# Scores cut from two PSUM banks by ScalarE, probabilities turned by VectorE alone, and a second square on ScalarE, in an attention-and-MLP kernel

## The chip, the cores and the metric

The kernel runs on one core of one Trainium2 chip. The metric is the device time of one execution in microseconds (us); the median over several runs counts.

## What is computed

Attention of 4 batches, 8 heads, 576 positions, head size 64, then two MLPs on the 2304 tokens, all in float32:

```python
scores = scale * np.matmul(q, k.transpose(0, 1, 3, 2))
rel = pos[:, None] - pos[None, :]
mask_local = (rel >= 0) & (rel < stride)                 # heads 0 to 3, stride = 32
mask_strided = (rel >= 0) & (pos[None, :] % stride == pos[:, None] % stride)   # heads 4 to 7
scores = np.where(masks[None, :, :, :], scores, -1000000000.0)
scores = scores - np.max(scores, axis=-1, keepdims=True)
attn = np.exp(scores)
attn = attn / (np.sum(attn, axis=-1, keepdims=True) + 1e-09)
x = np.matmul(attn, v)                                   # to 2304 tokens of 512
r = np.maximum(x @ w_in, 0.0); x = (r * r) @ w_out       # MLP 1, 512 -> 2048 -> 512
h = x @ w_in; g = h / (1.0 + np.exp(-1.702 * h)); out = g @ w_out      # MLP 2
```

A query of a local head sees at most 32 keys, a query of a strided head at most 18.

## The kernel before

**Attention.** The masks are used: the work is cut into 28 groups of 8 heads' or rows' worth of small score matrices. A strided group holds eight matrices in which 4 x 18 queries meet 4 x 18 keys, of which only the four 18 x 18 blocks on the diagonal count. A local group holds eight matrices of 96 queries by 128 keys, of which a query sees 32. Seven groups make a batch: four strided, three local. Groups 14 to 17 and 21 to 24 are strided, 18 to 20 and 25 to 27 local. Per group: `load` (DMA of q, k, v), `att_turn` (transposes of q and k into `qkT`), `att_S` (eight pairs of matmuls into two PSUM banks `ps_att`), mask and maximum (`att_max`), exponential (`att_exp`), division by the sum (`att_norm`), transposition of the probabilities, and `att_PV`, whose result goes through casts (L563, L566) into the MLP's input `xr`.

From group 14 (`n >= NTR`) q and k are turned on DVE. A strided group's scores are masked by eight DVE instructions that read PSUM (L401), and its probabilities are turned by four DVE transposes (L472) into a zeroed tile `pt`. A local group's scores are masked by eight custom DVE instructions (L421) that also give the maxima, its exponentials are eight ACT instructions (L443) that also give the sums, and its probabilities are turned by eight PE transposes (`att_P`, L483) into PSUM and copied out by two DVE copies (L493).

**MLP 1.** Each float32 operand is split in a high and a low part of PE's fast type, so a product is three matmuls. Tokens come in blocks `i` of 512, 512, 256, 512 and 512; the hidden layer in 16 steps `f`. A step is 12 matmuls into `ps_h` (L583), then the activation: ACT takes the relu (`t`, L612) and its square rounded to the high part (`gh`, L613), then `t` is squared once more (DVE, L617; ACT at L615 once `lpool` exists, from block 3), and DVE subtracts to get the low part (`gl`, L618). One step later `second` does 8 matmuls with `gh` and 4 with `gl` into the four banks `ps_acc` (L645). `t` has one buffer, `gh` and `gl` two; the two `ps_h` banks are shared with `att_PV`. At the end of blocks 0 and 1 `spill_x2` copies the four `ps_acc` banks (L700: banks 0 and 2 by DVE, 1 and 3 by ACT) into one tile with two places, and each copy leaves by a DMA; banks 2 and 3 wait for the DMAs of banks 0 and 1.

**Order.** Groups 0 to 13 and block 0 are in a hand-written front part. Groups 14 to 27 lie within the 32 steps of blocks 1 and 2: a table `AT` gives for each group the step of its scores, of its transposition and of its PV (group 18: steps 8, 9, 10; group 26: 24, 26, 28). In these blocks PE runs in program order, while DVE, ACT, GpSimd (POOL) and SyncE (SP) are put in order by a scheduler. From step (3, 0) PE, DVE and ACT run in program order. Blocks 3 and 4 also prepare the weights of MLP 2, which are loaded by DMA from then on; MLP 2 follows.

Of the kernel before, what the change touches and what calls it, by code (L numbers as in the profile page):

```python
# [22 lines left out]
def kernel(  # L23
# [176 lines left out]
    mloc = apool.tile([QT, 2, P], F32, name="mloc")  # L200
    mstr = apool.tile([SR, SR], F32, tag="mstr", name="mstr", bufs=1)
    mtri = []
# [26 lines left out]

    def shape(n):  # L230

        R, N = rows(groups[n][1])
        return (P, N, P) if n >= NTR and N == SR else (R, N, P)

# [141 lines left out]
    def att_S(n, tag, z=0):  # L376
        b, c, g = groups[n]
        R, N, _ = shape(n)
        ps = [bank(tag), bank(tag)]
        idle(ps[0], z)  # L380
        for j in range(4):
            qT, kT = tiles_qk(n, j)
            for i in range(2):
                d = slice(i * D, (i + 1) * D)
                nc.tensor.matmul(ps[i][0:R, j * P:j * P + N], qT[d], kT[d], start=True, stop=True)  # L385
        g_t[n] = ps

    def att_max(n):
        b, c, g = groups[n]
        R, N, step = shape(n)  # L390
        ps = g_t[n]
        if R == P:

            pr = abuf(n, [P, 8 * P], "pr", 1, 3)[:, 0:8 * 32].rearrange("p (x k) -> p x k", x=8)
            st = abuf(n, [P, 2, 8], "st", 1, 3)
            nc.gpsimd.memset(pr, 0.0)
            for i in range(2):
                s = ps[i].rearrange("p (j k) -> p j k", j=4)
                for r in range(4):
                    p, k0 = slice(32 * r, 32 * (r + 1)), NS * r  # L400
                    nc.vector.tensor_tensor(  # L401
                        out=pr[p, 4 * i:4 * i + 4, 0:NS], in0=s[p, :, k0:k0 + NS],
                        in1=mtri[0][p].unsqueeze(1).to_broadcast([32, 4, NS]), op=ALU.add,
                    )
            x, m = pr[:, :, 0:NS], st[:, 0, :]
            nc.vector.tensor_reduce(out=m, in_=x, op=ALU.max, axis=mybir.AxisListType.X)
            nc.vector.tensor_tensor(out=x, in0=x, in1=m.unsqueeze(2).to_broadcast([P, 8, NS]), op=ALU.subtract)
            g_t[n] = [pr, st, None]
            return
        pr = abuf(n, [P, 8 * P], "pr", 1, 3)[0:R, 0:8 * step].rearrange("p (i j k) -> p i j k", i=2, j=4)  # L410
        st = abuf(n, [P, 2, 8], "st", 1, 3)
        for j in range(4):
            for i in range(2):
                x = 4 * i + j
                if c >= 2:
                    m = mstr
                elif n < NTR:
                    m = mloc[:, 0 if g == 0 and i == 0 else 1, :]
                else:
                    m = mloc[:, 0 if (g, j) in ((0, 0), (1, 2)) else 1, :]  # L420
                nc.vector.tensor_tensor_reduce(  # L421
                    out=pr[:, i, j, 0:N], in0=ps[i][0:R, j * P:j * P + N], in1=m,
# [5 lines left out]
    def load_tri():  # L428
        mtri.append(apool.tile([P, SR], F32, tag="mstr", name="mtri", bufs=1)[:, 0:NS])
        nc.gpsimd.memset(mtri[0], -BIG)  # L430
        for r in range(0, P, 32):
            nc.sync.dma_start(mtri[0][r:r + NS], c_mstr.rearrange("(p r) (x y) -> r y p x", r=4, y=4)[0, 0])

    def att_exp(n, js=range(4)):
        R, N, _ = shape(n)
        pr, st, _ = g_t[n]
        if R == P:
            nc.scalar.activation(pr[:, :, 0:NS], pr[:, :, 0:NS], AF.Exp, scale=SCALE)
            return
        for j in js:  # L440
            for i in range(2):
                x = 4 * i + j
                nc.scalar.activation(  # L443
                    pr[:, i, j, 0:N], pr[:, i, j, 0:N], AF.Exp,
# [3 lines left out]
    def att_norm(n):  # L448
        R, N, _ = shape(n)
        pr, st, _ = g_t[n]  # L450
        if R == P:
            p = pr[:, :, 0:NS]
            N = NS
            nc.vector.tensor_reduce(out=st[:, 1, :], in_=p, op=ALU.add, axis=mybir.AxisListType.X)
        else:
            p = pr.rearrange("p i j k -> p (i j) k")[:, :, 0:N]
        nc.vector.tensor_scalar_add(st[0:R, 1, :], st[0:R, 1, :], 1e-9)
        nc.vector.reciprocal(st[0:R, 1, :], st[0:R, 1, :])
        nc.vector.tensor_tensor(
            out=p, in0=p, in1=st[0:R, 1, :].unsqueeze(2).to_broadcast([R, 8, N]), op=ALU.mult,  # L460
        )

    def att_turn_p(n):


        pr = g_t[n][0]
        pt = apool.tile([P, 2, DM], F32, tag="tmp0", name="pt", bufs=1).rearrange("p a n -> p (a n)")
        pt = pt.rearrange("p (x r k) -> p x r k", x=8, r=4)
        nc.gpsimd.memset(pt, 0.0)
        for r in range(4):  # L470
            p = slice(32 * r, 32 * (r + 1))
            nc.vector.transpose(pt[p, :, r], pr[p])  # L472
        g_t[n][2] = pt

    def att_P(n, tag, z=0):
# [20 lines left out]
    def att_PV(n, tag, z=0):  # L496
# [819 lines left out]
```

## Time and profile before

| | |
|---|---|
| median of 3 runs | 875.06 us (874.41 to 876.12) |
| profiled execution, its own time | 874.62 us |
| its span in the profile | 872.9 us |
| mean granted clock of PE | 0.999 of full speed |
| PE busy | 852.2 us, 98% of the span |
| DVE busy | 644.0 us, 74% |
| ACT busy | 462.7 us, 53% |
| POOL busy | 24.3 us, 3% |

The span is what the profile covers of the execution; the 1.7 us beside it lie around it. Times in the rows are microseconds from the span's start. Blocks 1 and 2, in which groups 14 to 27 are worked on, begin at 155.13 (first matmul L583 of step (1, 0)) and end at 328.42 (first matmul of step (3, 0)).

### The profile page before, as it was taken

How to read it: one execution, taken by the hardware profiler on the slowest of the kernel's cores; microseconds unless marked ns; L12 is line 12 of the kernel's file. 1: busy time of each engine (PE TensorE's matmuls, PEld its weight loads, DVE VectorE, ACT ScalarE, POOL GpSimd, SP SyncE). 2: the span in 40 equal slices, each digit the busy share in tenths (PEclk: the TensorE clock that was granted, in tenths of full speed). 3: DMA queues.
4: the chain of work that ended last, by engine and by line, in shares of the span. 5: the costliest groups of instructions: out<-in, count | busy, mean ns of one | idle time of the engine just before them, and what ended most of it. 6: DMA issues, size and time to landing. Idle time of an engine off the chain costs nothing.

```text
span 872.9 us, 15792 instructions
## 1 busy us (share of the span) xinstructions
PE 852.2 (98%) x5675; PEld 759.3 (87%) x5681; DVE 644.0 (74%) x1314; ACT 462.7 (53%) x1015; POOL 24.3 (3%) x49
## 2 busy tenths in 40 slices
PE   8999999999999999999989999999999999999998
PEld 5678787788888888888867899999999999999998
DVE  5999996776679656777858768788546797356853
ACT  7988896223522435555636645555344555344442
POOL 0000001110111000000000000000000000000000
PEclk9999999999999999999999999999999999999999
DMA  8997321222123206888888589987998597986673
GB/s 206 303 318 240 61 40 28 77 47 46 35 48 93 48 2 203 267 265 264 305 321 287 179 281 395 382 277 246 313 352 252 161 335 263 349 272 204 198 252 106
DMA packets 173508, 181.58 MB, mean 208 GB/s; under 512 B 71192, under 2 KB 128504, under 8 KB 171896
## 3 DMA queue, kind: packets, MB, share of 16 engines
q1 hardware_dynamic: 173432, 180.59, 64.9%
q8 instruction: 45, 0.74, 0.3%
q14 instruction: 31, 0.25, 0.1%
HBM read 141.75 MB, written 38.80 MB: 207 GB/s over the span
## 4 chain that ended last, share of the span: by engine, by line
PE 73%; DMA 11%; DVE 9%; ACT 3%; issue 1%; SPq 1%; POOL 0%; DVEq 0%; ACTq 0%
PE ps_acc L645 17%; PE ps_h L583 16%; PE ps_acc L1086 15%; PE ps_att L851 9%; PE ps_h L1086 6%; PE ps_h L851 5%; DMA stg<-in_moe_w_out_dram 4%; DMA stage<-in_moe_w_out_dram 2%; PE ps_acc L851 2%; DMA stg<-in_moe_w_in_dram 2%; PE ps_att L385 2%; ACT pr L443 1%; DVE tmp L154 1%; PE ps_h L507 1%; DVE tmp L158 1%
## 5 line engine op out<-in xcount | busy, mean ns | idle before, releaser
L583 PE MATMUL ps_h<-xr,whl 128*128 128x512 f32 (+1 forms) x948 | 211.2, 371 | 0.0
L583 PEld LDWEIGHTS ps_h<-xr,whl 128*128 128x128 f32 x948 | 164.4, 188 | 31.4 <-DVE whl L187 0.5
L645 PE MATMUL ps_acc<-gh,whl 128*128 128x512 f32 (+1 forms) x640 | 147.5, 372 | 5.0 <-ACT gh L613 2.8
L645 PEld LDWEIGHTS ps_acc<-gh,whl 128*128 128x128 f32 x640 | 111.3, 189 | 26.5 <-ACT gh L613 3.9
L645 PE MATMUL ps_acc<-gl,whl 128*128 128x512 f32 (+1 forms) x320 | 79.2, 369 | 2.6 <-DVE gl L618 2.6
L612 ACT ACTIVATE t<-ps_h 128x512 f32<-128x512 f32 (+1 forms) x64 | 34.6, 540 | 84.0 <-PE ps_h L583 73.1
L622 ACT ACTIVATE gh<-hs 128x384 f32<-128x384 f32 x72 | 37.8, 525 | 63.3 <-DVE hs L1022 63.3
L645 PEld LDWEIGHTS ps_acc<-gl,whl 128*128 128x128 f32 x320 | 56.6, 188 | 13.6 <-DVE gl L618 3.6
L443 ACT ACTIVATE pr<-pr,st 96x128 f32<-96x128 f32 (+1 forms) x160 | 59.4, 380 | 8.7 <-DVE st L421 8.7
L851 PE MATMUL ps_att<-xop,wst 128*128 128x384 f32 x288 | 58.8, 338 | 0.2
L851 PE MATMUL ps_att<-xop 128*128 128x384 f32 x288 | 58.1, 336 | 0.3 <-ACT hs L1030 0.3
L1086 PE MATMUL ps_acc<-misc,gop 128*128 128x256 f32 x432 | 54.2, 283 | 0.0
L1022 DVE TENSOR_TENSOR hs<-ps_h,hs 128x384 f32<-128x384 f32 x49 | 27.2, 556 | 35.4 <-ACT hs L1030 24.5
L1086 PEld LDWEIGHTS ps_acc<-misc,gop 128*128 128x128 f32 x432 | 53.2, 191 | 0.0
L1072 ACT CAST gop<-misc 128x768 fp32r<-128x768 f32 x42 | 34.7, 834 | 34.6 <-PE ps_acc L1086 19.0
L1072 ACT CAST gop<-g 128x768 fp32r<-128x768 f32 x42 | 34.8, 834 | 34.1 <-PE ps_acc L1086 19.8
L1025 DVE TENSOR_TENSOR gop<-g,gop 128x768 fp32r<-128x768 f32 x42 | 40.2, 956 | 16.9 <-ACT gop L1072 16.9
L851 PEld LDWEIGHTS ps_att<-xop,wst 128*128 128x128 f32 x288 | 51.0, 187 | 0.9 <-ACT hs L1030 0.9
L851 PEld LDWEIGHTS ps_att<-xop 128*128 128x128 f32 x288 | 50.4, 188 | 1.3 <-ACT hs L1030 1.2
L771 ACT CAST wst<-tmp 128x1792 fp32r<-128x1792 f32 x14 | 23.7, 1695 | 50.9 <-DVE tmp L757 43.0
L1025 DVE TENSOR_TENSOR gop<-misc,gop 128x768 fp32r<-128x768 f32 x42 | 39.9, 957 | 13.8 <-ACT gop L1072 13.7
L774 DVE TENSOR_TENSOR wst<-tmp,wst 128x1792 fp32r<-128x1792 f32 x14 | 28.4, 2025 | 26.0 <-ACT wst L771 26.0
(150 smaller groups left out, 1485.2 us busy)
## 6 DMA issues: line engine op xcount, KB each, us to landing
xop<-w2d SPq DMA_DIRECT2D x84, 256.0 KB
wst<-w2d SPq DMA_DIRECT2D x84, 256.0 KB
xop<-wo2d SPq DMA_DIRECT2D x63, 256.0 KB
w2d<-wst SPq DMA_DIRECT2D x16, 896.0 KB
misc<-wo2d SPq DMA_DIRECT2D x12, 1024.0 KB
wo2d<-wst SPq DMA_DIRECT2D x12, 896.0 KB
wx<-wo2d SPq DMA_DIRECT2D x36, 256.0 KB
stg<-in_moe_w_in_dram SPq DMA_DIRECT2D x16, 512.0 KB
```

Of the source, the lines that this page charges most:

```text
L443: nc.scalar.activation(pr[:, i, j, 0:N], pr[:, i, j, 0:N], AF.Exp, bias=st[0:R, 0, x:x + 1], scale=-1.0, accum_out=st[0:R, 1, x:x + 1],)
L583: nc.tensor.matmul(ph[:, 0:nb], w[:, kk * P:(kk + 1) * P], x[:, kk], start=(kk == KS[0] and w is ih and x is xh), stop=(kk == KS[-1] and x ...
L612: nc.scalar.activation(t, ph[:, 0:nb], AF.Relu)
L622: nc.scalar.activation(t, h, AF.Sigmoid, scale=1.702)
L645: nc.tensor.matmul(acc[c][:, 0:nb], w[:, c * P:(c + 1) * P], x, start=(f == 0 and w is oh and not lo), stop=(f == NF - 1 and lo == 1),)
L771: nc.scalar.copy(wh[:, x], t[:, x])
L774: nc.vector.tensor_tensor(out=wl[:, x], in0=t[:, x], in1=f32(wh)[:, x], op=ALU.subtract)
L851: nc.tensor.matmul(ps[:, 0:NH], w[:, a, k * P:(k + 1) * P], x[:, b + k], start=start and y == 0, stop=y == len(prods) - 1, skip_group_chec ...
L1022: nc.vector.tensor_tensor(out=h, in0=ps, in1=h, op=ALU.add)
L1025: nc.vector.tensor_tensor(out=out, in0=a, in1=b, op=op)
L1072: nc.scalar.copy(hi, g)
L1086: nc.tensor.matmul(part(ps, m), g, w[1 + h], start=j in (0, 1, 3) and p == 0 and m != 1 and not last and h == 0, stop=p == NP - 1 and last ...
```

## The change

For groups 14 to 27 the path from scores to turned probabilities is new. The two banks of scores are one tile (`bank2`). `att_cut`: ACT copies from both banks at once the block of keys that a set of 32 queries can see (strided: four copies of 32 x (8 x 18), local: three copies of 32 x (8 x 64)) into `pr`. `att_soft`: DVE adds a mask (`mwin`, loaded by eight DMAs), takes the maxima and subtracts them; one ACT instruction takes the exponentials; DVE sums, adds 1e-9, takes reciprocals and multiplies. `att_turn_p`: one DVE transpose turns all 32 x 32 blocks, and ACT copies them (strided four, local six copies) into the zeroed tile `pt`, from other partitions than those to which they go. PE turns no probabilities of these groups any more, and PE's score matmul of a strided group has 114 instead of 128 stationary columns. `att_turn(n + 1)` and `load(n + 2)` stand at the end of the step instead of in its middle. The second square of block 1 is done by ACT. The pair of `ps_att` banks is one tile in groups 0 to 13 as well, and two tiles again from step (3, 0).

```diff
+    def bank2(tag):
+        if tag == "att":
+            t = pool2.tile([P, 2, 512], F32, tag="att", name="ps_att", bufs=1)
+            pairs[:] = [t]
+            return [t[:, 0], t[:, 1]]
+        return [bank(tag), bank(tag)]
...
     def att_S(n, tag, z=0):
         b, c, g = groups[n]
-        R, N, _ = shape(n)
-        ps = [bank(tag), bank(tag)]
+        R, N = rows(c)
+        if n >= NTR and c >= 2:
+            R = 3 * 32 + NS
+        ps = bank2(tag)
...
+    def window(n):
+        if groups[n][1] >= 2:
+            return NS, 32, P, P, [(slice(32 * r, 32 * r + (32 if r < 3 else NS)), NS * r) for r in range(4)]
+        return 64, 64, QT, QT, [(slice(32 * a, 32 * a + 32), 32 * a) for a in range(3)]
...
+    def att_cut(n):
+        W, room, _, _, blocks = window(n)
+        t = apool.tile([P, 2, 8 * 64], F32, tag="pr", name="pr", bufs=1)[:, :, 0:8 * room]
+        t = t.rearrange("p o (x k) -> p o x k", x=8)
+        pr = t[:, 0]
+        s = pairs[0].rearrange("p i (j k) -> p (i j) k", j=4)
+        if room > W:
+            nc.gpsimd.memset(pr, 0.0)
+        for p, k0 in blocks:
+            nc.scalar.copy(pr[p, :, 0:W], s[p, :, k0:k0 + W])
+        g_t[n] = t
+
+    def att_soft(n):
...
+        each(mwin[c >= 2][0:R].unsqueeze(1).to_broadcast([R, 8, W]), ALU.add)
+        if c < 2 and g < 2:
+            nc.vector.memset(pr.rearrange("p (i j) k -> p i j k", i=2)[0:32, :, 2 * g, 0:32], -BIG)
+        nc.vector.tensor_reduce(out=m, in_=x, op=ALU.max, axis=mybir.AxisListType.X)
+        each(row(m), ALU.subtract)
+        nc.scalar.activation(x, x, AF.Exp, scale=SCALE)
+        nc.vector.tensor_reduce(out=z, in_=x, op=ALU.add, axis=mybir.AxisListType.X)
+        nc.vector.tensor_scalar_add(z, z, 1e-9)
+        nc.vector.reciprocal(z, z)
+        each(row(z), ALU.mult)
...
     def att_turn_p(n):
-        pr = g_t[n][0]
+        W, room, R, nq, _ = window(n)
+        pr, tu = (g_t[n][0:R, o].rearrange("p x k -> p (x k)") for o in range(2))
+        nc.vector.transpose(tu, pr)
+        tu = tu.rearrange("p (x e q) -> p x e q", x=8, q=32)
         pt = apool.tile([P, 2, DM], F32, tag="tmp0", name="pt", bufs=1).rearrange("p a n -> p (a n)")
-        pt = pt.rearrange("p (x r k) -> p x r k", x=8, r=4)
+        pt = pt[:, 0:8 * nq].rearrange("p (x q) -> p x q", x=8)
         nc.gpsimd.memset(pt, 0.0)
-        for r in range(4):
-            p = slice(32 * r, 32 * (r + 1))
-            nc.vector.transpose(pt[p, :, r], pr[p])
-        g_t[n][2] = pt
+        w = min(W, 32)
+        for a in range(0, nq, 32):
+            for e in range(room // 32):
+                k = a + 32 * e
+                nc.scalar.copy(pt[k:k + 32, :, a:a + w], tu[a:a + 32, :, e, 0:w])
+        g_t[n] = pt
...
-        if lpool:
+        if lpool or i == 1:
             nc.scalar.activation(t, t, AF.Square)
...
             for n in steps[0]:
                 att_S(n, "att")
-                att_max(n)
+                att_cut(n)
             ph = bank("h")
             mm_h(i, f, ph, KS)
             for n in steps[0]:
-                att_exp(n)
-                att_norm(n)
-                if n + 1 < len(groups):
-                    att_turn(n + 1)
-                    load(n + 2)
+                att_soft(n)
             for n in steps[1]:
-                if groups[n][1] >= 2:
-                    att_turn_p(n)
-                else:
-                    att_P(n, "att")
-                    att_pt(n, [nc.vector.tensor_copy] * 2)
+                att_turn_p(n)
...
             second(*prev)
             prev = (i, f)
+            for n in steps[0]:
+                if n + 1 < len(groups):
+                    att_turn(n + 1)
+                    load(n + 2)
```

How this moves instructions is seen at three places. In these rows a line number is that of the kernel named, `x12` a count, and `out<-in` the tiles; L615, L677 and L538 of the changed kernel are L583, L645 and L507 of before.

First, PE in block 1, around the PV of the first local group (18). Before:

```order
L583 MATMUL ps_h<-xr,whl 128x512 x12
L483 MATMUL ps_att<-ident,pr 128x96 x8
L645 MATMUL ps_acc<-gh,whl 128x512 x8
L645 MATMUL ps_acc<-gl,whl 128x512 x4
L507 MATMUL ps_h<-pr,ldv 64x96 x8
L385 MATMUL ps_att<-qkT 96x128 x8
L583 MATMUL ps_h<-xr,whl 128x512 x12
```

And now:

```order
L615 MATMUL ps_h<-xr,whl 128x512 x12
L677 MATMUL ps_acc<-gh,whl 128x512 x8
L677 MATMUL ps_acc<-gl,whl 128x512 x4
L538 MATMUL ps_h<-pt,ldv 64x96 x8
L395 MATMUL ps_att<-qkT 96x128 x8
L615 MATMUL ps_h<-xr,whl 128x512 x12
```

The eight transposes into `ps_att` between a step's `ps_h` and `ps_acc` matmuls are gone, and the PV follows the `ps_acc` matmuls of the step directly.

Second, ACT in block 1, around the same kind of group. Before, with eight exponentials ahead of a relu:

```order
L443 ACTIVATE pr,st<-pr,st 96x128 x8
L612 ACTIVATE t<-ps_h 128x512
L613 ACTIVATE gh<-t 128x512
L612 ACTIVATE t<-ps_h 128x512
L613 ACTIVATE gh<-t 128x512
```

And now, for one local group from its cut (L462) to its copies into `pt` (L503), with the relu L644, the rounded square L645 and the second square L647 of the steps between:

```order
L462 COPY pr<-ps_att 32x512 x3
L644 ACTIVATE t<-ps_h 128x512
L645 ACTIVATE gh<-t 128x512
L483 ACTIVATE pr<-pr 96x512
L647 ACTIVATE t<-t 128x512
L644 ACTIVATE t<-ps_h 128x512
L503 COPY pt<-pr 32x8x32 x6
L645 ACTIVATE gh<-t 128x512
```

The six copies into `pt` stand behind the relu of the step at whose end PV needs them, and ahead of that step's squares.

Third, the end of block 1 on DVE, where the `ps_acc` banks are copied away. Before:

```order
L617 TENSOR_TENSOR t<-t 128x256
L618 TENSOR_TENSOR gl<-t,gh 128x256
L700 COPY tmp<-ps_acc 128x512
L401 TENSOR_TENSOR pr<-ps_att,mtri 32x4x18 x8
L312 STREAM_TRANSPOSE qkT<-ld 128x2x4x4x32
L406 TENSOR_REDUCE st<-pr 128x8
L700 COPY tmp<-ps_acc 128x512
```

And now:

```order
L649 TENSOR_TENSOR t<-t 128x256
L732 COPY tmp<-ps_acc 128x512
L650 TENSOR_TENSOR gl<-t,gh 128x256
L320 STREAM_TRANSPOSE qkT<-ld 128x2x4x4x32
L732 COPY tmp<-ps_acc 128x512
```

The copy of bank 0 has moved ahead of the subtraction that gives `gl`, and the eight masks that stood between the copies of banks 0 and 2 are gone. ACT now has its four cuts between banks 1 and 3 there:

```order
L645 ACTIVATE gh<-t 128x256
L732 COPY tmp<-ps_acc 128x512
L462 COPY pr<-ps_att 32x8x18 x3
L462 COPY pr<-ps_att 18x8x18
L732 COPY tmp<-ps_acc 128x512
```

Before, these two copies stood next to each other, and no instruction of ACT lay between them.

## Rows read from the trace of the kernel before

**Rows 1.** view by stretch: us, busy us of each engine (instructions), PEclk granted clock, DMA share, GB/s

```profile
154.00:328.00 174.00, 168.89 (x1260) 144.41 (x1260) 123.60 (x377) 61.27 (x200) 17.64 (x33) 1.00 0.24 50
328.00:620.00 292.00, 287.59 (x1541) 254.44 (x1541) 226.16 (x300) 164.21 (x241) 0.00 (x0) 1.00 0.83 285
```

**Rows 2.** waits of PE from 150 to 335: total us, times, longest us

```profile
PE ps_acc L645 <- ACT tmp L700: 1.5, 1, 1.5
PE ps_acc L645 <- DVE gl L618: 1.5, 2, 0.8
PE ps_att L483 <- DVE pr L459: 1.5, 1, 1.5
PE ps_acc L645 <- DVE tmp L700: 0.6, 2, 0.4
```

**Rows 3.** timeline of PE in block i=1: start us, us, line, tiles, count

```profile
202.39 1.98 PE L645 MATMUL ps_acc<-gh,whl 128*128 128x512 f32 x8
204.21 1.07 PE L645 MATMUL ps_acc<-gl,whl 128*128 128x512 f32 x4
212.48 2.88 PE L583 MATMUL ps_h<-xr,whl 128*128 128x512 f32 x12
215.20 0.82 PE L483 MATMUL ps_att<-ident,pr 96*128 96x96 f32 x8
215.81 2.08 PE L645 MATMUL ps_acc<-gh,whl 128*128 128x512 f32 x8
217.73 1.07 PE L645 MATMUL ps_acc<-gl,whl 128*128 128x512 f32 x4
218.73 0.88 PE L507 MATMUL ps_h<-pr,ldv 128*64 128x96 f32 x16
219.54 1.12 PE L385 MATMUL ps_att<-qkT 64*96 64x128 f32 x16
```

**Rows 4.** timeline of PE where group 14 begins

```profile
147.10 0.39 PE L519 MATMUL ps_h<-pr,ldv 128*64 128x96 f32 x4
147.41 0.44 PE L385 MATMUL ps_att<-qkT 64*128 64x72 f32 x2
147.78 0.72 PE L519 MATMUL ps_h<-pr,ldv 128*64 128x96 f32 x12
148.43 2.11 PE L645 MATMUL ps_acc<-gh,whl 128*128 128x512 f32 x8
```

**Rows 5.** timeline of DVE before PE's wait that ends at 291.72

```profile
289.69 1.21 DVE L459 TENSOR_TENSOR pr<-pr,st 96x1024 f32<-96x1024 f32 x1
...
291.26 0.41 DVE L618 TENSOR_TENSOR gl<-t,gh 128x256 fp32r<-128x256 f32 x1
```

**Rows 6.** timelines of DVE and ACT at the end of block i=1

```profile
265.92 0.43 DVE L618 TENSOR_TENSOR gl<-t,gh 128x256 fp32r<-128x256 f32 x1
266.26 0.68 DVE L700 COPY tmp<-ps_acc 128x512 f32<-128x512 f32 x1
...
269.50 0.59 ACT L700 COPY tmp<-ps_acc 128x512 f32<-128x512 f32 x1 [3.88 <-DMA x2d<-tmp]
```

**Rows 7.** DVE by line and shape, 81 to 335: busy us, mean ns of one

```profile
L401 DVE TENSOR_TENSOR pr<-ps_att,mtri 32x72 f32<-32x72 f32 x64 | 14.7, 229 | 3.9 <-PE ps_att L385 2.8
L617 DVE TENSOR_TENSOR t<-t 128x512 f32<-128x512 f32 x16 | 11.0, 688 | 5.3 <-ACT gh L613 5.2
L472 DVE STREAM_TRANSPOSE pt<-pr 32x256 f32<-32x256 f32 x32 | 13.9, 435 | 1.2 <-POOL pt L469 0.5
```

**Rows 8.** ACT by line and shape, 81 to 335, and one pair of copies

```profile
L443 ACT ACTIVATE pr<-pr,st 96x128 f32<-96x128 f32 x72 | 27.9, 390 | 7.5 <-DVE st L421 7.5
L612 ACT ACTIVATE t<-ps_h 128x512 f32<-128x512 f32 x17 | 10.1, 593 | 49.9 <-PE ps_h L583 49.9
L613 ACT ACTIVATE gh<-t 128x256 fp32r<-128x256 f32 x16 | 6.7, 416 | 0.4
...
129.94 0.83 ACT L493 COPY pr<-ps_att 128x384 f32<-128x384 f32 x2
```

More of the change, by code (lines that the diff above doesn't have):

```diff
@@ L199 @@
     ident = apool.tile([P, P], F32, name="ident")
[L200 to L202 removed]
+    mloc = apool.tile([QT, 2, P], F32, tag="mloc", name="mloc", bufs=1)
+    mstr = apool.tile([SR, SR], F32, name="mstr")
     zeros = []
@@ L228, in rows @@
         return (QT, P) if c < 2 else (SR, SR)
-    def shape(n):
-        R, N = rows(groups[n][1])
-        return (P, N, P) if n >= NTR and N == SR else (R, N, P)
     def load(n):
@@ L377, in att_S @@
         b, c, g = groups[n]
-        R, N, _ = shape(n)
-        ps = [bank(tag), bank(tag)]
+        R, N = rows(c)
+        if n >= NTR and c >= 2:
+            R = 3 * 32 + NS
+        ps = bank2(tag)
         idle(ps[0], z)
@@ L384, in att_S @@
                 d = slice(i * D, (i + 1) * D)
-                nc.tensor.matmul(ps[i][0:R, j * P:j * P + N], qT[d], kT[d], start=True, stop=True)
+                nc.tensor.matmul(ps[i][0:R, j * P:j * P + N], qT[d][:, 0:R], kT[d], start=True, stop=True)
         g_t[n] = ps
@@ L389, in att_max @@
         b, c, g = groups[n]
-        R, N, step = shape(n)
+        R, N = rows(c)
         ps = g_t[n]
[L392 to L398, printed above, removed]
-                for r in range(4):
[L400 to L410, printed above, removed]
+        pr = abuf(n, [P, 8 * P], "pr", 1, 3)[0:QT].rearrange("p (i j k) -> p i j k", i=2, j=4)
         st = abuf(n, [P, 2, 8], "st", 1, 3)
@@ L426, in att_max @@
         g_t[n] = [pr, st, None]
[L428 to L432, printed above, removed]
     def att_exp(n, js=range(4)):
-        R, N, _ = shape(n)
+        R, N = rows(groups[n][1])
         pr, st, _ = g_t[n]
-        if R == P:
-            nc.scalar.activation(pr[:, :, 0:NS], pr[:, :, 0:NS], AF.Exp, scale=SCALE)
-            return
         for j in js:
@@ L448, in att_norm @@
     def att_norm(n):
-        R, N, _ = shape(n)
+        R, N = rows(groups[n][1])
         pr, st, _ = g_t[n]
[L451 to L461, printed above, removed]
+        z = st[0:R, 1, :]
@@ new lines, with load_masks @@
+    mwin = []
+    def load_masks():
+        t = apool.tile([P, NS + 64], F32, tag="mloc", name="mwin", bufs=1)
+        nc.gpsimd.memset(t, -BIG)
+        for r in range(0, P, 32):
+            nc.sync.dma_start(t[r:r + NS, 0:NS], c_mstr.rearrange("(p r) (x y) -> r y p x", r=4, y=4)[0, 0])
+            nc.sync.dma_start(t[r:r + 32, NS:NS + 64], c_mloc[0:32, 1, 0:64])
+        mwin.extend((t[:, NS:NS + 64], t[:, 0:NS]))
+    def att_cut(n):
[9 more added lines that the diff above has]
+        g_t[n] = t
@@ new lines, in att_soft, with each, row @@
+    def att_soft(n):
+        W, _, R, _, _ = window(n)
+        _, c, g = groups[n]
+        pr, st = g_t[n][:, 0], apool.tile([P, 2, 8], F32, tag="st", name="st", bufs=1)
+        x, m, z = pr[0:R, :, 0:W], st[0:R, 0], st[0:R, 1]
+        def each(y, op):
+            nc.vector.tensor_tensor(out=x, in0=x, in1=y, op=op)
+        def row(y):
+            return y.unsqueeze(2).to_broadcast([R, 8, W])
+        each(mwin[c >= 2][0:R].unsqueeze(1).to_broadcast([R, 8, W]), ALU.add)
[5 more added lines that the diff above has]
+        nc.vector.tensor_reduce(out=z, in_=x, op=ALU.add, axis=mybir.AxisListType.X)
+        nc.vector.tensor_scalar_add(z, z, 1e-9)
+        nc.vector.reciprocal(z, z)
+        each(row(z), ALU.mult)
@@ L478, in att_P @@
         pr, st, _ = g_t[n]
-        ps = [bank(tag), bank(tag)]
+        ps = bank2(tag)
         idle(ps[0], z)
@@ L916, in table_step @@
                 fetch(n)
-    ps = bank("att")
-    idle(ps, 8)
+    idle(bank2("att")[0], 8)
     for word in FRONT.split():
@@ L951 @@
                 att.close()
+                paired.close()
+                pool1.append(ctx.enter_context(
+                    tc.tile_pool(name="psum1", bufs=1, space=bass.MemoryType.PSUM, reuse_waits="tile")))
                 lpool = ctx.enter_context(tc.tile_pool(name="lpool", bufs=1, side="right", reuse_waits="tile"))
```

32 lines of the change are left out of this document (17 added, 15 removed).

## The prediction

> **What bounds the kernel now.** I read the busy times by stretch first: the reader is to see that from 154 to 328, where groups 14 to 27 run beside blocks 1 and 2, PE is busy for 168.89 of 174 us, DVE for 123.60 and ACT for only 61.27, and that from 328 to 620 PE is busy for 287.59 of 292 [rows 1]. PE's clock is at its upper level throughout, 1.00 of 2.4 GHz, so no term here comes from the clock. PE therefore sets the time in both stretches, and a change in the first one counts only where it takes matmuls from PE or ends a wait of PE. Second I read PE's waits there: 5.1 us in four lines, all behind ACT or DVE [rows 2]. Third the timeline of PE over a step with and one without probabilities to turn [rows 3], and the place where group 14 begins [rows 4]. Last, what stood ahead of the instruction that PE waited for [rows 5, 6].
>
> **What it takes away from PE.** A local group's eight PE transposes begin at 215.20 and the next matmuls at 215.81: 0.61 us. The eight matmuls behind them start slower as well, 215.81 to 217.73 is 1.92 where 202.39 to 204.21 is 1.82 [rows 3]. That makes 0.71 per group, for six groups (18 to 20, 25 to 27) **-4.3 us**. The work that takes their place is on DVE and ACT; what it costs if it is late is the first rival.
>
> The waits of PE in block 2 go: twice 1.5 us in all for `gl`, once 1.5 for group 26's probabilities [rows 2]. Their cause is that the multiplication of 96x1024, 1.21 us, stands ahead of `gl` on DVE [rows 5], and that eight exponentials of 0.390, 3.1 us, occupy ACT ahead of the relu or the square [rows 8]. Now a local group multiplies 512 elements (0.688 for that many in L617, [rows 7]) and takes one exponential, by the 512-element relu 0.593 [rows 8]. **-3.0 us**; if one of the three waits stays in another form, -2.
>
> At the end of block 1 PE waits 1.5 for ACT's copy of a bank, which had waited for the DMA of DVE's copy, and up to 0.4 for DVE's next one [rows 2, 6]. DVE's copy of bank 0 began at 266.26, behind `gl` at 265.92 [rows 6]; now it stands ahead of `gl`, 0.34 earlier, and with it its DMA and ACT's copy. The eight masks (0.229 each, 1.8 us, [rows 7]) between DVE's two copies are gone, so the second one no longer comes after ACT's. 0.34 and 0.4 make **-0.7**. If the DMA decides alone, it is -0.3.
>
> Before, two score matmuls of group 14 stood inside the PV of group 13: that piece took 147.10 to 148.43, 1.33 [rows 4], where a PV of the same shape takes 218.73 to 219.54, 0.81 [rows 3]. Two of sixteen such matmuls cost at most 0.14 in one piece (1.12 for sixteen, [rows 3]), so the cut cost 1.33 - 0.81 - 0.14: **-0.4**. Nothing else than PE's order is behind it; bounds 0 and -0.5.
>
> **What it adds.** Per local group ACT now has three cuts of 512 (0.593 each by the relu from PSUM), one exponential of 512 and six copies of 256; per strided group four cuts and four copies of 144. In block 1 it has 16 more squares, some 0.6 each. It loses 48 exponentials, 18.7 us. With 0.4 for each copy of 144 the sum is 10.7 + 3.6 + 15 + 25.6 + 9.6 - 18.7, about 46 us more on 61 of 174: ACT stays under two thirds, and on average nothing happens. DVE loses more than it gets.
>
> What decides is one place. For groups 18 to 20 the six copies into `pt` stand on ACT behind the relu of a step, and PV stands on PE behind that step's `ps_acc` matmuls. From the end of `ps_h` to PV PE has 1.82 + 1.00 = 2.82 us of work (202.39 to 204.21, and 217.73 to 218.73, [rows 3]). In it ACT must do the relu, 0.593, and six copies of c, with 0.1 for the last one's end and the hand-over. PV waits if 0.69 + 6c is above 2.82, that is for c above 0.355. No copy from SBUF between partitions stands in the trace. The nearest row is the rounded square of 256 elements, SBUF to SBUF, 0.416 alone; consecutive copies overlap: two of 384 take 0.83 together, and one, between 0.416 for 256 and 0.593 for 512, about 0.50, so the second starts some 0.33 after the first [rows 8]. With an overlap of at least 0.1 c is 0.31, and PV does not wait: **0**. Without any overlap c is 0.416 and PV waits 0.37 per group; twice the row is the far bound.
>
> The rule that speaks against the change is in the Trainium skill, "ScalarE: Activation LUTs", section "Rules for kernel authors": simple arithmetic belongs on VectorE, which it puts at up to about three times ScalarE's rate per element in bf16. The rows of this kernel, all float32, show no such gap: 0.688 on DVE against 0.593 on ACT for 512 elements [rows 7, 8]. By that rule a copy of 256 elements would cost ACT up to three times half of 0.688, about 1.0 (an estimate from the page's factor), and 6 x (0.69 + 6 - 2.82), some 23 us, would turn the sum into a loss; by the rows the sum stays as it is. It is rival 2 at its far end.
>
> The other new wait is the chain of a local group: cuts 3 x 0.593, three DVE operations of 0.688 by L617 and two sums of as much, a transpose of 512 of under 0.87 (twice L472), an exponential, 0.4 of small ones: 1.8 + 3.4 + 0.9 + 0.6 + 0.4 = 7.1 [rows 7, 8], and `gl` of the step beside it, 0.7. From the scores to the copies there are two `ps_h` of 2.72 (212.48 to 215.20), one `ps_acc` of 2.82 and a relu, 8.9 [rows 3]. So about 1 us is to spare: 0.
>
> ACT's copy of bank 1 at the start of block 1 now stands behind the four copies of group 14: **+0.2**, at most 1. The pair of banks is one tile in the front part too, so a transposition waits for both readers: **+0.1**, bounds 0 and 0.5. The eight mask loads and the later `load(n + 2)` stand on SP's queue ahead of data that are needed two steps on: 0. The 114 instead of 128 stationary columns leave the 72 moving ones as they are: 0.
>
> **Sum.** -4.3 - 3.0 - 0.7 - 0.4 + 0.2 + 0.1 = -8.1. From step (3, 0) on everything shifts: PE is busy for 98% of the stretch, and its loads start when the attention's pool closes there. On the profiled execution, 874.62, this gives 866.5; the median of the runs, 875.06, lies 0.4 above it. I say 866.8.
>
> **The rivals.**
> 1. *The copies between partitions are a little dearer.* At c = 0.416, PV waits 0.37 in three groups, and in block 2, where the copies stand ahead of `gh` in steps half as long, as much again in three: 2.2 us, 869.0. For it: no row shows the operation. Against: ACT's other copies overlap.
> 2. *Slower.* The same place, with copies at a different price: 6 x (0.69 + 6c - 2.82) eats 8.1 from c = 0.58. At c = 0.65 the loss is 10.6, and the time 877.4. For it: they cross partitions, in a quarter of the lanes. Against: the rows give 0.416 for a whole 128 partitions and nothing that adds 0.2.
> 3. *Only the transposes go.* The three waits of block 2 come back as waits on the hand-overs between ACT and DVE, which are in order: an exponential now waits for DVE with the relu of the next step behind it, and PE waits for that relu's bank. The gain is 4.3 + 0.7 + 0.4 - 0.3, the time 869.8. For it: seven hand-overs per group where there were three. Against: about 1 us to spare in the chain.
> 4. *The gain is lost behind 328.* There the DMA is busy for 0.83 [rows 1]. If its loads did not start earlier with PE, half of the gain would be lost: 870.8. Against: PE has under 5 us of idle time there, so it is PE that the loads keep up with.
>
> **Chances and numbers.** The forecast (865.0 to 868.0) 0.58; rival 1 0.15, rival 3 0.10, rival 4 0.05; rival 2 0.07; the rest, 0.05, is that several of these cancel to within 0.2%, about what a measurement of this kernel can tell from no change (1.75 us: 873.3 to 876.8). So faster 0.88, same 0.05, slower 0.07. The range reaches from 864.8 (all bounds of the gains met, without the 0.3 added) to 870.8, over rivals 1, 3 and 4.
>
> **What would show it.** No matmul line with an identity and `pr` after 155; the steps of groups 18 to 20 at 5.5 us like the strided ones; no wait of PE for `gl` in block 2; a wait at the end of block 1 of about 1.2. The six copies of 256 at a start-to-start time of 0.31, and no wait of PE's PV for `pt`. The first matmul of step (3, 0), at 328.4 before, at about 320.3, and the end as much earlier. The prediction is wrong if the copies take over 0.355 each, if PE waits for `ps_h` banks behind an exponential, or if the shift at 328 is not kept to the end.

## The result and the profile after

The changed kernel takes 865.4 us (median of four runs, 864.65 to 867.22) against 875.12: ratio 0.9891, 95% interval 0.9872 to 0.9910, that is 7.9 to 11.2 us less. Six more runs on another occasion gave 865.24 and a ratio of 0.9881 (0.9860 to 0.9902). The prediction was 866.8, range 864.8 to 870.8. The profiled execution has a span of 862.9, 10.0 less than before, at a granted clock of 1.00.

The stretch of [rows 1] after the change (columns as there):

```profile
154.00:328.00 174.00, 171.43 (x1259) 146.99 (x1258) 95.11 (x215) 103.59 (x252) 21.93 (x39) 1.00 0.26 58
```

PE is fuller, DVE has lost 28 us and ACT has won 42 in the same 174 us, whose last 8 are already block 3 in the changed kernel. PE's waits from 150 to 330, where [rows 2] had 5.1 us (total us, times, longest us):

```profile
PE ps_h L538 <- issue: 1.4, 4, 0.4
PE ps_acc L677 <- ACT tmp L732: 0.8, 1, 0.8
PE ps_h L615 <- ACT t L644: 0.4, 1, 0.4
```

The waits for `gl` and for the probabilities of group 26 are gone, that for the copied banks has shrunk from 2.1 to 0.8. New are four waits ahead of PV (L538), for which the view names no engine, and one for a relu. The place of [rows 3] in the changed kernel, timeline of PE around group 18's PV and then of ACT beside it:

```profile
214.08 1.98 PE L677 MATMUL ps_acc<-gh,whl 128*128 128x512 f32 x8
215.89 1.07 PE L677 MATMUL ps_acc<-gl,whl 128*128 128x512 f32 x4
217.33 0.88 PE L538 MATMUL ps_h<-pt,ldv 128*64 128x96 f32 x16 [0.37 <-issue]
```

```profile
214.28 0.60 ACT L644 ACTIVATE t<-ps_h 128x512 f32<-128x512 f32 x1 [2.99 <-PE ps_h L615]
214.77 2.46 ACT L503 COPY pt<-pr 32x256 f32<-32x256 f32 x6
217.25 0.63 ACT L645 ACTIVATE gh<-t 128x512 fp32r<-128x512 f32 x1
```

The transposes between `ps_h` and `ps_acc` are no longer there. The six copies end at 217.23, 0.1 before PV starts. They took 2.46 at a mean of 0.402 (the next group of rows), so each starts (2.46 - 0.402) / 5 = 0.411 after the one ahead: no overlap. PV itself starts 1.44 after `gl`'s matmuls where it started 1.00 after them [rows 3], so the wait of 0.37 costs 0.44. ACT by line and shape, 154 to 330 (busy us, mean ns of one):

```profile
L503 ACT COPY pt<-pr 32x256 f32<-32x256 f32 x36 | 14.5, 402 | 3.0 <-DVE pr L494 2.7
L462 ACT COPY pr<-ps_att 32x512 f32<-32x512 f32 x18 | 10.4, 577 | 2.0 <-PE ps_att L395 1.8
```

Where the 8.75 us up to step (3, 0) came from is read from the start of each step's first `ps_h` matmul in the timelines of PE:

| first matmul of step | before | changed | gained so far | what lies in between |
|---|---|---|---|---|
| (1, 0) | 155.13 | 154.75 | 0.38 | group 14's scores in one piece, front part |
| (1, 1) | 160.72 | 160.32 | 0.40 | |
| (1, 2) | 168.48 | 167.54 | 0.94 | end of block 0, scores of group 15 |
| (1, 9) | 212.48 | 211.36 | 1.12 | scores of two strided groups |
| (1, 14) | 247.96 | 245.93 | 2.03 | groups 18, 19, 20 |
| (2, 1) | 266.42 | 264.19 | 2.23 | scores of two strided groups |
| (2, 2) | 272.57 | 268.91 | 3.66 | end of block 1 |
| (2, 3) | 276.67 | 272.93 | 3.74 | scores of one strided group |
| (3, 0) | 328.42 | 319.67 | 8.75 | rest of block 2: groups 25, 26, 27 |

### The profile page after: what moved, and what is told of

Its sections match the earlier page's. It is cut to its first block, busy times and chain, and to the rows that moved or that the text cites. A ratio compares the mean times of both kernels' runs of the same rounds, so it can differ in the third digit from the quotient of the medians.

```text
span 862.9 us, 15613 instructions
## 1 busy us (share of the span) xinstructions
PE 846.8 (98%) x5633; PEld 754.4 (87%) x5633; DVE 611.0 (71%) x1144; ACT 500.2 (58%) x1059; POOL 28.6 (3%) x55
## 4 chain that ended last, share of the span: by engine, by line
PE 48%; DVE 10%; ACT 5%; issue 4%; DMA 3%; SPq 0%; ACTq 0%; DVEq 0%
PE ps_acc L1116 15%; PE ps_att L883 10%; PE ps_h L1116 6%; PE ps_h L883 5%; PE ps_acc L677 5%; PE ps_h L615 5%; PE ps_acc L883 2%; DVE tmp L168 2%; DVE tmp L172 2%; ACT tmp L778 2%; DVE tmp L789 1%; DMA stage<-in_moe_w_out_dram 1%; DVE tmp L163 1%; DVE tmp L161 1%; DVE gl L650 1%
## 5 line engine op out<-in xcount | busy, mean ns | idle before, releaser
L615 PE MATMUL ps_h<-xr,whl 128*128 128x512 f32 (+1 forms) x948 | 211.6, 372 | 1.2 <-DVE whl L201 0.8
L615 PEld LDWEIGHTS ps_h<-xr,whl 128*128 128x128 f32 x948 | 164.3, 188 | 32.9 <-DVE whl L201 1.6
L677 PE MATMUL ps_acc<-gh,whl 128*128 128x512 f32 (+1 forms) x640 | 146.4, 371 | 2.5 <-ACT gh L645 1.8
L677 PEld LDWEIGHTS ps_acc<-gh,whl 128*128 128x128 f32 x640 | 111.6, 189 | 23.8 <-ACT gh L645 2.8
L677 PE MATMUL ps_acc<-gl,whl 128*128 128x512 f32 (+1 forms) x320 | 78.9, 369 | 1.0 <-DVE gl L650 1.0
L650 DVE TENSOR_TENSOR gl<-t,gh 128x512 fp32r<-128x512 f32 (+1 forms) x64 | 39.6, 619 | 44.3 <-ACT t L647 43.9
L677 PEld LDWEIGHTS ps_acc<-gl,whl 128*128 128x128 f32 x320 | 56.7, 189 | 11.6 <-DVE gl L650 1.7
L644 ACT ACTIVATE t<-ps_h 128x512 f32<-128x512 f32 (+1 forms) x64 | 34.7, 543 | 47.8 <-PE ps_h L615 42.6
L1060 ACT COPY hs<-ps_att 128x384 f32<-128x384 f32 x72 | 33.7, 472 | 25.4 <-PE ps_att L883 24.6
```

The source lines that it names most:

```text
L615: nc.tensor.matmul(ph[:, 0:nb], w[:, kk * P:(kk + 1) * P], x[:, kk], start=(kk == KS[0] and w is ih and x is xh), stop=(kk == KS[-1] and x ...
L644: nc.scalar.activation(t, ph[:, 0:nb], AF.Relu)
L650: nc.vector.tensor_tensor(out=gl, in0=t, in1=f32(gh), op=ALU.subtract)
L677: nc.tensor.matmul(acc[c][:, 0:nb], w[:, c * P:(c + 1) * P], x, start=(f == 0 and w is oh and not lo), stop=(f == NF - 1 and lo == 1),)
L1060: nc.scalar.copy(hs[:, n], X[:, 0:NH])
```

## The experiments

From here on "the distance" is the time from the first matmul of step (1, 0) to that of step (3, 0): 173.29 before, 164.92 in the changed kernel and 164.93 in its second profile. It leaves out what the front part and the part behind 328 do from one execution to the next. It does hold what a lower clock of PE costs inside it: in three of the profiles (experiments 3 and 5 and the second one of experiment 6) the granted clock fell there for some microseconds, to 0.50 of 2.4 GHz, which is the lower level of 1.2; in all others it stayed at 1.00.

**1. 128 stationary columns again in the strided groups' scores.**

```diff
-            R = 3 * 32 + NS
+            R = P
```

> The changed kernel with 128 stationary columns again in the score matmuls of the eight strided groups (114 in the change). In the changed kernel eight pairs of them take 0.95 us where they took 1.05. Theory: these matmuls are paced by the number of stationary columns, so each of the eight groups takes 1.05 again and the first matmul of step (3, 0) comes 0.8 later, at 320.4 instead of 319.67. Rival: the 72 moving columns pace them and the 0.1 comes from the one tile for both banks; then 0.95 stays and step (3, 0) begins at 319.7.

Measured: eight times 1.04 to 1.05 instead of 0.95 from the score matmuls to the next matmul. The distance grew to 166.31: 0.64 by the seven score pieces that lie in it and 0.75 by a wait for a relu in step (2, 9), behind a DVE turn that had waited 2.23 for a DMA in this execution. Step (3, 0) came at 324.40 because the front part was 3.3 late (last section); this single run took 869.64. The score matmuls by shape, of the changed kernel and of this one (stationary, then moving; busy us, mean ns):

```profile
L395 PE MATMUL ps_att<-qkT 64*114 64x72 f32 x128 | 8.2, 266 | 0.0
```

```profile
L395 PE MATMUL ps_att<-qkT 64*128 64x72 f32 x128 | 8.9, 278 | 0.0
```

The 72 moving columns and the one tile for both banks are the same in both, so the stationary columns make the difference, and 14 fewer of them are worth 0.1 per group. The theory holds.

**2. The local groups' copies on DVE.**

```diff
-                nc.scalar.copy(pt[k:k + 32, :, a:a + w], tu[a:a + 32, :, e, 0:w])
+                (nc.scalar.copy if W == NS else nc.vector.tensor_copy)(
+                    pt[k:k + 32, :, a:a + w], tu[a:a + 32, :, e, 0:w])
```

> The changed kernel with the six copies of a local group into the zeroed tile done by VectorE instead of ScalarE. Theory: PE's waits ahead of the PV of groups 18, 19, 20 (0.37 each) and 27 (0.30), and for the relu behind group 26's copies (0.40), come from ScalarE's copies, which start 0.41 apart behind a relu. On VectorE they can start when the transpose is done, about 0.8 earlier, so all these waits go: step (3, 0) begins 1.8 earlier than 319.67, at 317.9, and the time is about 863.6. Rival: PV waits for something else (GpSimd's zeroing, the DMA of v; the profile names no engine for these four); then step (3, 0) stays at 319.7 and the time at 865.4.

Measured: 862.68 (862.33 to 864.5), ratio to the kernel before 0.9860 (0.9843 to 0.9877); distance 162.79, 2.13 less than in the changed kernel. One wait of PE is left in the stretch, and group 18's PV follows at once. Waits of PE, then the timelines of DVE and of PE, and DVE's line:

```profile
PE ps_acc L678 <- ACT tmp L733: 0.8, 1, 0.8
```

```profile
213.35 0.71 DVE L494 STREAM_TRANSPOSE pr<-pr 96x512 f32<-96x512 f32 x1
214.16 1.77 DVE L503 COPY pt<-pr 32x256 f32<-32x256 f32 x6
...
215.97 1.07 PE L678 MATMUL ps_acc<-gl,whl 128*128 128x512 f32 x4
216.97 0.88 PE L539 MATMUL ps_h<-pt,ldv 128*64 128x96 f32 x16
...
L503 DVE COPY pt<-pr 32x256 f32<-32x256 f32 x36 | 10.2, 283 | 0.7
```

DVE does a copy in 0.283 and six in 1.77, beginning when the transpose is done and not behind a relu. So PV had waited for ACT's copies. This kernel is shorter than both others in the distance and in the median, though the interval of its ratio overlaps a little with the changed kernel's (0.9872 to 0.9910).

**3. Each copy twice on ACT.** The copy that experiment 2 takes out (first line of its edit) stands twice for local groups.

> The changed kernel with each of the six copies of a local group done twice by ScalarE (same data). Theory: six more copies 0.41 apart are 2.5 us; PV of groups 18 to 20 waits 2.8 each instead of 0.37, and block 2 loses 4 to 7 us: step (3, 0) begins between 331 and 334 and the gain over the kernel before is gone. Rival: the copies are not what PV waits for; step (3, 0) moves by under 1 us.

Measured: distance 187.74, a single run of 888.01. PE waits 17.5 us ahead of PV, six times; group 18:

```profile
216.03 1.07 PE L679 MATMUL ps_acc<-gl,whl 128*128 128x512 f32 x4
220.61 0.88 PE L540 MATMUL ps_h<-pt,ldv 128*64 128x96 f32 x16 [3.52 <-issue]
```

3.52 instead of 0.37: the six further copies took 2.5, and the scheduler put a step's `gh` (0.63) between the two sets. The direction is the theory's, the size beyond its bounds (22.8 us against 11 to 14). Of the 22.8, 16.1 are longer waits ahead of PV, more than foreseen in block 2, where steps are half as long (0.89, 3.04 and 4.52 there). Another 6.3 are slower matmuls: with the waits of 3.52, 3.52 and 4.52 PE's granted clock fell, with those of 0.89, 2.01 and 3.04 it did not. The rest is a wait of 0.4 for `gl`. The stretches from group 20's PV on and from group 26's on (columns as in [rows 1]):

```profile
253.80:262.00 8.20, 8.19 (x49) 6.90 (x50) 4.83 (x11) 2.90 (x9) 2.64 (x4) 0.65 0.17 35
322.50:331.00 8.50, 8.50 (x80) 8.38 (x81) 6.82 (x17) 4.83 (x13) 0.74 (x1) 1.00 0.01 2
```

**4. The second square of block 1 back on DVE.**

```diff
-        if lpool or i == 1:
+        if lpool:
```

> The changed kernel with the second square of block 1 back on VectorE. Theory: nobody on PE's path waits for that square, neither ScalarE (60% busy) nor VectorE (55%) is full there; step (3, 0) stays at 319.7 within 0.3 and the time within 0.5 of 865.4. Rival: VectorE's chain of a local group (scores to turned probabilities), which has some 0.8 to spare, is delayed by 0.69 in each of two steps, and PV of groups 18 to 20 waits up to 0.6 longer each: 321 to 321.5, 867.

Measured: 866.92 (866.1 to 868.73), distance 165.61, 0.69 more than in the changed kernel. Nearly all of it (0.67) arises at one place that neither the theory nor the rival had named, the end of block 0: ACT and then PE,

```profile
163.94 0.63 ACT L645 ACTIVATE gh<-t 128x512 fp32r<-128x512 f32 x1
164.48 0.57 ACT L732 COPY tmp<-ps_acc 128x512 f32<-128x512 f32 x1
...
165.10 0.73 PE L677 MATMUL ps_acc<-gh,whl 128*128 128x512 f32 x2 [0.47 <-ACT tmp L732]
```

ACT's last copy of a bank stands behind `gh` here and came ahead of it in the changed kernel. The scheduler chose that place; the square decides it. Groups 18 to 20 did not wait longer.

**5. Only the local groups on the new path** (strided ones by the old eight masks and four transposes, inside `att_cut`, `att_soft` and `att_turn_p`; 128 stationary columns):

```diff
     def att_cut(n):
         W, room, _, _, blocks = window(n)
+        if W == NS:
...
+            for i in range(2):
+                s = pairs[0][:, i].rearrange("p (j k) -> p j k", j=4)
+                for r in range(4):
+                    p, k0 = slice(32 * r, 32 * (r + 1)), NS * r
+                    nc.vector.tensor_tensor(
+                        out=t[p, 4 * i:4 * i + 4, 0:NS], in0=s[p, :, k0:k0 + NS],
+                        in1=mwin[1][p].unsqueeze(1).to_broadcast([32, 4, NS]), op=ALU.add,
+                    )
```

> The changed kernel with only the local groups on the new path: strided groups are masked, exponentiated and turned as before the change (eight masks and four transposes on VectorE, 128 stationary columns). Theory, parts add: the six groups' PE transposes (-4.3) and the waits of block 2 (-3.0) go, the new waits ahead of PV stay (+1.8); the gains at the ends of blocks 0 and 1 and of the narrower scores do not come. Step (3, 0) begins near 322.6 (328.42 before, 319.67 changed), the time is about 869.5. Rival: the waits of block 2 went because the strided groups left VectorE; then they come back and step (3, 0) begins at 325 or later, 872.

Measured: 867.79 (866.99 to 868.9), ratio 0.9906; distance 169.16, step (3, 0) at 323.91. From step (2, 3) on it gains 5.02 us, the changed kernel 5.01; over groups 18 to 20, 0.81, the changed kernel 0.91 with 0.1 of one strided group's scores. So these parts are the local groups' alone, and the rival falls. What is missing against the theory is at the block ends: against the kernel before, 0.63 is lost at the end of block 0 and 1.07 at that of block 1, where DVE's second copy again stands behind masks and a turn (DVE, then PE):

```profile
266.05 1.93 DVE L464 TENSOR_TENSOR pr<-ps_att,mwin 32x72 f32<-32x72 f32 x8 [0.42 <-PE ps_att L395]
268.01 1.25 DVE L320 STREAM_TRANSPOSE qkT<-ld 128x1024 f32<-128x1024 f32 x1
269.28 0.69 DVE L769 COPY tmp<-ps_acc 128x512 f32<-128x512 f32 x1
...
270.03 0.50 PE L714 MATMUL ps_acc<-gh,whl 128*128 128x256 f32 x2 [1.63 <-DVE tmp L769]
...
271.82 2.93 PE L652 MATMUL ps_h<-xr,whl 128*128 128x256 f32 x12
```

The wait of 1.63 is shorter than the two of the kernel before together (1.5 and 0.4). The loss is PE's clock in this profile: behind the wait it fell, the twelve `ps_h` matmuls took 2.93 where they take 1.70 in the kernel before, and from PV's start (270.94) to the `gl` matmuls (275.56) it was 4.62 where the kernel before needs 3.14. Two microseconds of it (columns as in [rows 1]):

```profile
272.00:274.00 2.00, 2.00 (x10) 2.00 (x11) 1.38 (x5) 0.40 (x2) 1.38 (x2) 0.50 0.21 38
```

Without these 1.5, step (3, 0) would have come at about 322.4 (an estimate, 323.91 - 1.5), where the theory had 322.6; that it fits so well is in part luck, since 0.6 lost at the end of block 0 and 0.4 won at that of block 1 are both outside the theory.

**6. Only the strided groups on the new path** (local ones masked, exponentiated eight times and turned by PE as before; the mask tiles and the operand of PV follow, not shown):

```diff
                 att_S(n, "att")
-                att_cut(n)
+                if groups[n][1] >= 2:
+                    att_cut(n)
+                else:
+                    att_max(n)
...
-                att_turn_p(n)
+                if groups[n][1] >= 2:
+                    att_turn_p(n)
+                else:
+                    att_P(n, "att")
+                    att_pt(n, [nc.vector.tensor_copy] * 2)
```

> The changed kernel with only the strided groups on the new path: local groups are masked on VectorE, take eight exponentials, and are turned by PE as before the change. Theory, parts add: the narrower scores (-0.8), the piece at the start of group 14 (-0.4) and the ends of blocks 0 and 1 (-0.5 and -1.4) are gained, PE's transposes and the waits of block 2 stay: step (3, 0) begins near 325.4, the time is about 872.0. Rival: the waits of block 2 (3.0) go too, since VectorE has less to do: 322.4, 869.

> The kernel with only the strided groups on the new path, a second look. In its first profile the copy of a spilled bank waited until 4.0 us after its place's DMA was issued, where the changed kernel waited 2.8, and PE lost 2.4 at the end of block 1 instead of 0.8. Theory: that landing was an accident of that execution; now PE waits about 0.8 there, and from step (1, 0) to step (3, 0) it takes 170.5 instead of 172.2 (before 173.3, changed 164.9). Rival: the order of instructions in this kernel makes the DMA late; then 2.4 and 172.2 come again.

Measured: 874.25 in ten runs (871.84 to 877.79), ratio 0.9989 (0.9973 to 1.0005), no difference that can be told; distance 172.18, and 173.61 in a second profile (a single run of 874.07). The narrower scores came, and block 2's waits stayed, 1.3 for `gl` and 1.5 for group 26, so the rival of the first expectation falls. But at the end of block 1 PE waits 2.4 in the first profile and 2.5 in the second. From the second, ACT and PE:

```profile
269.23 0.59 ACT L736 COPY tmp<-ps_acc 128x512 f32<-128x512 f32 x1 [2.72 <-DMA x2d<-tmp]
...
269.87 1.22 PE L681 MATMUL ps_acc<-gh,whl 128*128 128x256 f32 x4 [2.49 <-ACT tmp L736]
```

From these matmuls to the next step's first one it took 3.16 in the second profile and 1.79 in the first, and that is nearly all of the 1.4 between the two distances: behind 2.49 of waiting the granted clock fell, behind 2.36 it did not. The same two microseconds, first and second profile:

```profile
270.00:272.00 2.00, 2.00 (x28) 1.79 (x27) 1.73 (x7) 0.67 (x3) 0.75 (x2) 1.00 0.59 168
270.00:272.00 2.00, 2.00 (x10) 1.78 (x12) 1.32 (x5) 0.73 (x3) 0.00 (x0) 0.50 0.51 154
```

The accident that I had expected to vanish came again, which speaks for the rival of the second expectation: this kernel's own order makes the wait for the DMA long. Why ACT waits 2.72 here (2.59 in the first profile) and copies 4.5 us after the first DMA's issue, where the changed kernel's ACT waited 0.99 and copied after 2.8, although all issued the two DMAs within 0.83, no run settles.

**7. The kernel before with only the second square of block 1 on ACT** (the condition of experiment 4, put into the kernel before).

> The kernel before with only the second square of block 1 on ScalarE. Theory: the square matters at one place, the end of block 0, where VectorE's copy of a bank no longer stands behind it (-0.4 to -0.7 us); elsewhere nobody waits for it. Step (1, 0) to step (3, 0) takes 172.7 (173.3 before), and the time is the same as before. Rival: ScalarE, which here also has eight exponentials per local group, delays the rounded square, and PE waits for it after groups 18 to 20: 174 or more.

Measured: 875.46 (873.15 to 878.21), ratio 1.0004 (0.9989 to 1.0019); distance 172.99. Gained: nothing at the end of block 0 (0.05), 0.25 at that of block 1: the theory's place was wrong, and the rival's wait does not occur. Alone the square is worth nothing that can be measured; in the changed kernel, taking it back costs 0.7 in the trace (experiment 4).

**8. The changed kernel again, and all copies into the zeroed tile on DVE.**

> The changed kernel once more, for the comparison with the next one on the same chip: 865.4 within 1. If the 0.9 that came behind step (3, 0) in its first profile belongs to the change, PE's longest wait for gh near 437 is 1.3 again; if it is the landing of DMAs, which differs from execution to execution, that wait lies anywhere from 1.3 to 2.5, as in the other kernels' profiles.

> The changed kernel with all copies into the zeroed tile on VectorE, those of the strided groups too. Theory: PE waits for none of the strided groups' copies, so this equals the kernel with only the local copies on VectorE: step (3, 0) at 317.6 within 0.3, 862.7; it is 2 us faster than the changed kernel beside it. Rival: ScalarE's copy of a spilled bank, which no longer stands behind group 14's or 22's copies, comes earlier, and PE's wait at the end of block 1 (0.8) shrinks: 317.0, 862. Other rival: VectorE's copies delay its subtraction for the low part, and PE waits for that: 318 to 320.

Measured: the changed kernel 865.24 (863.9 to 867.81), distance 164.93, PE's wait for `gh` near 437 is 1.05, a little under both that the expectation named. With all copies on DVE 863.05 (862.25 to 864.74), ratio 0.9858 (0.9837 to 0.9879), distance 162.45: 0.34 less than with the local copies alone, 0.3 of it at the end of block 1, where the wait is 0.5 instead of 0.8. That is the first rival's mechanism at half its size, and not to be told apart by the times (862.68 and 863.05). Against the changed kernel beside it, 865.24, that is 2.2 less; the intervals of the two ratios overlap, but in the distance, which came within 0.01 in the changed kernel's two profiles, both versions are shorter, by 2.1 and 2.5, all of these at a granted clock of 1.00 in the stretch; and the waits that are gone are seen in the traces.

## Why the prediction was right, point by point

The forecast was a sum of -8.1; up to step (3, 0) the profile shows -8.75, and the medians -9.7 with an interval that reaches from -7.9 to -11.2. The total is right, and in part by luck: the copies, put at 0, cost 2.1, and four other terms brought some 2.8 more than they were given (narrower scores 0.8, waits of block 2 and end of block 1 0.7 each, end of block 0 0.6). With these, -8.1 becomes -8.8.

Two things in the prediction itself do not hold. Its lower end, 864.8, is said to be all bounds of the gains met; but -4.3 - 3.0 - 0.7 - 0.5 is -8.5, some 866.4, and nothing in the sum reaches 1.6 lower, or the measured 865.4. And by its own sign, copies over 0.355 each, its mechanism was wrong at that place: they take 0.411.

- **PE transposes, -4.3: right.** With the copies on DVE, so that no wait hides it, groups 18 to 20 gain 2.26, of which 0.1 is one strided group's scores: 0.72 per group against 0.71.
- **Waits of block 2, -3.0: right in kind, a little small.** With the copies on DVE steps (2, 3) to (3, 0) gain 5.86; less 2.1 for three groups' transposes and 0.07 for a shorter PV of group 24 it is 3.7. Matmuls behind a wait also run slower: four `gl` matmuls took 0.74 at 320.41 and 291.72 and 0.64 elsewhere. Experiments 5 and 6 show that the term belongs to the local groups' new path.
- **The copies into `pt`, 0: this step failed.** It rested on c = 0.31, taken from pairs of 384 elements that overlap, copied from PSUM on 128 partitions [rows 8]. These copies do not: c is 0.411, and PV waits 0.37 in three groups, just what the working gave for "without any overlap" (0.37 per group at 0.416). Rival 1 was real; its price was 2.2, and experiment 2 gives back 2.13. That these agree is partly chance: it had six waits of 0.37, and there were four ahead of PV and one for a relu, which cost more each (experiment 2 wins 1.35 in groups 18 to 20 and 0.85 in block 2). Its 0.15 was too little: the nearest row by size was the rounded square of 256, 0.416, and the overlap came from another shape.
- **The rule weighed there.** The Trainium skill, "ScalarE: Activation LUTs", section "Rules for kernel authors", gives simple arithmetic such as adding and multiplying to VectorE, up to about three times faster per element in bf16; it does not name copies. I set it aside by rows for 512 elements, where ACT is no slower. For these float32 copies its direction was right, 0.283 on DVE against 0.402 on ACT for the same 32 x 256, a factor of 1.4; the price of 1.0 that the prediction worked out from it as an estimate was not met. On DVE the copies leave no wait of PE, while on ACT they cost 2.1.
- **114 instead of 128 stationary columns, 0: this step failed too.** It is worth 0.1 for each of eight groups, 0.8 in all (experiment 1). Weight loads of these matmuls took 176 ns for 114 columns and 187 for 128. The Trainium skill, "TensorE: Matmul & The Clock Gate", section "Back-to-back issue gap", says that spacing is set by the weight load and the matmul together; the run agrees, and I had counted the moving columns alone.
- **End of block 1, -0.7: too small.** It gained 1.43. The bound with the DMA alone deciding, -0.3, did not hold: bank 0's DMA went out with bank 1's, and DVE's second copy no longer stood behind the masks. With either half alone PE waits 1.6 or 2.4 there instead of 0.8 (experiments 5 and 6), so the full term belongs to the combination. The wait that stayed was forecast at about 1.2.
- **End of block 0, +0.2: wrong sign.** It gained 0.44. ACT's copy did stand behind four copies, but it was in time, and PE no longer waited there at all; experiment 4 shows how near the opposite was.
- **Group 14's start, -0.4, and the front's +0.1: right.** Together with 0.1 by narrower scores, 0.38 was gained at step (1, 0), although PE's transposes of group 13, ahead of it, began 0.21 later (143.54 against 143.33). No run puts `att_turn` and `load` back into the middle of the step, so what that move is worth by itself is not shown.
- **Everything behind shifts: right.** Step (3, 0) came 8.75 earlier, the end 10.0. The remaining 1.25 is not shown to be the change's. PE's first long wait behind 430, for `gh` behind a DMA, was 2.11 before, 1.26 changed and 2.53 with the local copies on DVE:

```profile
446.43 2.12 PE L645 MATMUL ps_acc<-gh,whl 128*128 128x512 f32 x8 [2.11 <-ACT gh L613]
```

```profile
436.82 2.11 PE L677 MATMUL ps_acc<-gh,whl 128*128 128x512 f32 x8 [1.26 <-ACT gh L645]
```

```profile
436.00 3.04 PE L678 MATMUL ps_acc<-gh,whl 128*128 128x512 f32 x8 [2.53 <-ACT gh L646]
```

From the first matmul of step (3, 0) to the end it was 544.5 us before, 543.2 and 543.5 in the two profiles of the changed kernel, and 545.1 with the local copies on DVE, so this part differs by as much as is to be explained. In the last one the granted clock was 0.66 from 436 to 441, behind the wait of 2.53 (the eight matmuls took 3.04 instead of 2.11); that profiled run took 864.50, the other three of its kernel 862.33 to 862.86.

- **Rivals 2, 3 and 4** did not come: c stayed below 0.58, the chain of a local group had its slack (the transpose ended 0.8 before the copies could begin), and the gain was kept behind 328.

## What to carry to other kernels

Where an in-order engine gets a burst of small instructions behind one that PE's path waits for, set the work PE has in hand against the burst at its full price; overlap measured on another shape is no price for it. Give such a burst to the engine that is free when its data are ready: the same copies cost 2.1 us on ScalarE and left no wait of PE on VectorE. In a program that keeps PE 98% busy, count the stationary columns of small matmuls too. And where two profiles differ by more than their waits, read the granted clock behind each long wait before naming another cause.

## What the runs showed of the hardware that was not expected

- ACT's consecutive copies on 32 partitions do not overlap: 0.411 from start to start at 0.402 each. The three cuts from PSUM on 32 partitions, 0.577 each, took 1.75 together, so they do not overlap either. The first copy did overlap with the relu ahead of it (214.28 + 0.60 is later than 214.77). Whether the partitions or something else decides, no run tells.
- PE's granted clock can fall behind a wait of a few microseconds and makes the wait dearer: 2.49 of waiting cost 1.4 more in experiment 6, 1.63 some 1.5 in experiment 5, three waits of 3.52 to 4.52 together 6.3 in experiment 3. Waits of 2.36 and 3.04 were followed by no fall, so the length of the wait alone does not tell.
- The same kernel's front part came 2.8 us later in its second profile, and 3.3 in experiment 1's. The stretches 20 to 40 and 40 to 60 of the changed kernel's two profiles (columns as in [rows 1]):

```profile
20.00:40.00 20.00, 18.77 (x208) 13.12 (x205) 19.62 (x83) 19.73 (x87) 0.00 (x0) 1.00 1.07 315
40.00:60.00 20.00, 18.96 (x158) 13.82 (x157) 19.79 (x63) 17.94 (x56) 0.30 (x1) 1.00 1.05 315
```

```profile
20.00:40.00 20.00, 16.79 (x180) 11.69 (x178) 19.62 (x83) 19.17 (x85) 0.00 (x0) 1.00 0.97 268
40.00:60.00 20.00, 19.53 (x163) 13.82 (x162) 17.13 (x59) 15.51 (x47) 0.00 (x0) 0.91 1.06 275
```

In the second one the DMAs moved 268 GB/s instead of 315, PE was busy for 2 us less, and in the next 20 us its granted clock was 0.91 of full speed. Of the 3.1 us between the two spans 2.8 arose there, so such starts are one reason why single times of one kernel lie up to 4 us apart. The distance between two steps leaves them out; with the clock inside it read beside it, it told experiments apart where the medians could not.
